# A gated mix of linear and softmax attention: where the heads' kv enters the output's weights

## The chip, the cores and the metric

The kernel runs on one core of a Trainium2 chip. The metric is the device time of one execution in microseconds (us), the median of several. The engines are TensorE (PE in the profile, with its weight loads as PEld), VectorE (DVE), ScalarE (ACT), GpSimd (POOL) and SyncE (SP), which issues every DMA of this kernel. A matmul multiplies a stationary operand, which a weight load puts into the array, with a moving operand of up to 512 columns, and writes one bank of PSUM (128 partitions by 512 numbers; there are eight).

## The reference

One input x of 2048 rows and 1024 columns goes through two attention blocks with 32 heads of 32 columns each, and a gate mixes the results:

```python
phi = lambda t: jnp.where(t > 0, t + 1, jnp.exp(t)) + 1e-6
# A: linear attention
kv = einsum("bhsd,bhse->bhde", phi(k), v)          # one 32x32 matrix for each head
z  = einsum("bhsd->bhd", phi(k))
a  = (einsum("bhqd,bhde->bhqe", phi(q), kv) / den) @ A_wo,   den = phi(q) . z + 1e-6
# B: softmax attention
b  = (softmax(q k^T * 32**-0.5) v) @ B_wo
g  = sigmoid((x * gate_w).sum(-1))
out = g * a + (1 - g) * b
```

In block A each head's kv stands between phi(q) and 32 rows of A_wo. So kv times those rows of A_wo is a matrix of weights that can be made once, and phi(q), divided by den and times g, is multiplied with it. Both the kernel before and the changed one do that. These weights are called the output's weights below: 1024 x 1024, made of 8 blocks of 128 rows (k), each holding four heads, in two halves of 512 columns (c).

## The kernel before

**Precision.** A large product is made of three: each operand is split into a high part (hi) rounded to fp32r and the rest (lo), and `three` (L145 to L150) issues hi*hi, hi*lo and lo*hi. ScalarE makes hi with a copy and VectorE or GpSimd makes lo with a subtraction. A few small products take plain fp32 instead, in one call.

**Stages.** First the value columns of B for half of the heads, then q and k of B for all heads, stored in DRAM (to L415), with the gate beside them (`gate`, L368, through the tile kvb) and x's parts spilled to DRAM. From there four streams share TensorE:

- `heads_` with `attend` (L868, L931): for each head 16 blocks of 128 keys by 4 column groups of 512 queries. A step is one product of scores (L902) and an exponential on ScalarE (L906). Groups of 5, 5 and 6 blocks are then multiplied with v (`av`, L982; L994: four matmuls for each block, whose outputs lie in four 32-partition groups of bank 4), and sums of the exponentials are kept by GpSimd (L951) and VectorE (L960).
- `maxima` (L738): the same scores in the other orientation (L752), whose row maxima VectorE takes (L757), about one head ahead.
- `linear` (L580): block A, in units of one 128-row tile with one chunk of columns: chunks v (the rest of B's values), kv (four), q (two) and o (two). A unit is 8 k-steps of three matmuls (L148 to L150). It yields to the other streams between matmuls. x's parts for a q unit or the q results (oA) for an o unit are loaded two units ahead (`load_xp`).
- `output` (L1078): block B's output product, at the end.

**Order.** The order on every engine is written out by hand: a planner in the kernel's own Python keeps a clock for each engine (`T`, with costs such as `MM` and `AV`), asks each stream when it could start, and advances the one that can start and is furthest behind. Six banks (`RING`) are handed out by `take` and `give`; VectorE work is deferred (`defer`) and filled in where the plan sees room (`fill`). `rates` (L1119 to L1125) paces `linear` against the heads' steps from the estimated cost of its chunks. SP takes the DMAs in the order of that plan and waits at each for what it depends on.

**The output's weights.** In the last unit of a chunk (tile NT-1) the weights of the next are put in place, k by k, as soon as the three matmuls on the old ones are issued: `split_w` (L444). For a q chunk they are loaded and split. For an o chunk `split_w` takes a bank, multiplies the block-diagonal 128x128 tile of four heads' kv with 128 rows of A_wo as one plain fp32 matmul (L455), copies hi from the bank (L457) and subtracts lo (L458), straight into the weights' place. That is 8 times in each of two hand-overs, from q to o and between the two o chunks. kv is summed in mid[8] during the kv chunks (`keys`, L493) and copied into the block-diagonal kvb by GpSimd after the last tile (L518), over zeros written at L635.

Of the kernel before, what the change touches and what calls it, by code (L numbers as in the profile page):

```python
# [9 lines left out]
F32 = mybir.dt.float32  # L10
# [35 lines left out]
def kernel(  # L46
# [35 lines left out]
    def f32r(ap):  # L82
# [13 lines left out]
    v_d = [dram.tile([P, NT, C], F32, name=f"v{c}") for c in range(NQC)]  # L96
    ra_d = [dram.tile([P, D], F32, name=f"ra{t}") for t in range(NT)]

    ident = sb.tile([P, P], F32, name="ident")
# [263 lines left out]

    HD = D // 2
    nc.sync.dma_start(zrep, bass.AP(tensor=gate_w.tensor, offset=gate_w.offset, ap=[[0, P], [1, D]]))
    kv_flat = kvb.rearrange("p k c -> p (k c)")

    def gate():  # L368
        for t in range(NT):
            for i in range(2):  # L370
                xn, junk = kv_flat[:, :HD], kv_flat[:, HD:]
# [51 lines left out]
    w_left = [[] for _ in range(NK)]  # L423
    xp_ready = [0.0, 0.0]
    oh, ol = f32r(mid[8]), f32r(mid[9])
    o_left = []
    k_left = []
    lin_done = [0.0]
    lin_kind = [chunks[0][0]]
# [1 line left out]
    def lin_pe(cost, *after):  # L431
        lin_done[0] += cost
        return use("pe", cost * MM, *after)

    def load_w(kind, c, k, n):
        if kind == "v":
            raw = load_cols(b_wqkv, vcols(c), k, n)
        elif kind == "kv":
            raw = load_cols(a_wqkv, [(D + c * HC, HC), (2 * D + c * HC, HC)], k, n)
        else:  # L440
            raw = load_cols(a_wqkv if kind == "q" else a_wo, [(c * C, C)], k, n)
        return raw, T["pe"] + 4.0

    def split_w(kind, c, k, raw, at, eng):  # L444

        hi, lo = wpart(k, 0), wpart(k, 1)
        w_left[k].clear()
        if kind == "o":
            yield from keys_alone(len(units))
            need(k_left)  # L450
            yield lambda: both(bank_at(), at)
            b = take()
            pb = bank[b]
            end = lin_pe(4.0, free[b])
            nc.tensor.matmul(pb, kvb[:, k, :], raw, start=True, stop=True)  # L455
            end = use("act", 0.5, end)
            nc.scalar.copy(hi, pb)  # L457
            item = defer(lambda _: nc.vector.tensor_sub(lo, pb, f32(hi)), end)  # L458
            give(b, 0.0, [item])
            w_left[k].append(item)  # L460
            return
        end = use("act", 0.52, at, T["pe"] + LATENCY["pe"])
        nc.scalar.copy(hi, raw)
        w_ready[k] = use("dve", 0.6, end) if eng is nc.vector else use("pool", 1.23, end)
        eng.tensor_sub(lo, raw, f32(hi))  # L465
# [22 lines left out]

    GC = HC // P
    kv_todo = deque()  # L490
    kv_acc = mid[8][:, :NK * DH].rearrange("p (k d) -> p k d", d=DH)

    def keys(n, c, t, pk, va, todo):  # L493

        def products(b, at):
            need(todo)
            lin_done[0] += 1.0
            end = use("pe", KV)  # L500
            pb = bank[b][:, at * GC * DH:(at + 1) * GC * DH]
            for g in range(GC):
                for r in range(4):
                    sl = slice(g * P + r * DH, g * P + (r + 1) * DH)
                    nc.tensor.matmul(pb[r * DH:(r + 1) * DH, g * DH:(g + 1) * DH], va[:, sl], pk[:, sl],  # L505
                                     start=True, stop=True)
            acc = kv_acc[:, c * GC:(c + 1) * GC, :]

            def total(_):
                part = pb.rearrange("p (k d) -> p k d", d=DH)  # L510
                if t == 0:
                    nc.vector.tensor_copy(acc, part)
                else:
                    nc.vector.tensor_add(acc, part, acc)
                if t == NT - 1:
                    for r in range(4):
                        rows = slice(r * DH, (r + 1) * DH)
                        nc.gpsimd.tensor_copy(kvb[rows, c * GC:(c + 1) * GC, rows], acc[rows])  # L518
# [16 lines left out]
    def keys_alone(n):  # L535

        while kv_todo and kv_todo[0][0] <= n:
            yield lambda: both(kv_todo[0][1](), bank_at()) if kv_todo else 0.0
            if kv_todo and kv_todo[0][0] <= n:
                use("pe", AV_SWITCH, kv_todo[0][1]())  # L540
                keys_now(T["pe"])

    z_end = [0.0, 0.0]

# [12 lines left out]
    def queries(n, c, t, pq, todo):  # L557
# [9 lines left out]
        end = use("act", 0.5, end)  # L567
        nc.scalar.copy(oh, pt)

        def low(_):  # L570
            nc.vector.tensor_sub(ol, pt, f32(oh))
            for p, src in enumerate((oh, ol)):
                nc.sync.dma_start(oA_d[p][t][:, c * TPC:(c + 1) * TPC, :],
                                  f32(src).rearrange("p (k c) -> p k c", c=P))
# [5 lines left out]
    def linear():  # L580
# [4 lines left out]
        for n, (i, t) in enumerate(units):  # L585
            kind, c = chunks[i]
            follow = chunks[i + 1] if i + 1 < len(chunks) else None
            xp = xp_t[n % 2]
            yield bank_at
# [10 lines left out]
            for k in range(NK):  # L600
# [3 lines left out]
                for m, _ in enumerate(three(ps, stat, (wpart(k, 0), wpart(k, 1)), k)):  # L604
                    lin_pe(1.0)
                    if m < 2:
                        yield always
                if k == 0 and kind == "v" and c == NQC - 1 and NT - 4 < t < NT - 1:
                    load_xp(n + 3)
                if k == 0 and n + 7 == len(units) and not o_main[0]:  # L610
# [4 lines left out]
                    split_o(1, slice(0, NK - 1))  # L615
                if k == NK - 1:
                    yield from extra
                if follow and t == NT - 2 and k < min(LEAD_W, NK):
                    coming_w.append(load_w(*follow, k, LEAD_W + 1))
                if follow and t == NT - 1:  # L620
                    yield from split_w(*follow, k, *coming_w.popleft(), nc.vector if kind == "v" else nc.gpsimd)
                    if k + LEAD_W < NK:
                        coming_w.append(load_w(*follow, k + LEAD_W, LEAD_W + 1))
            if n + 2 < len(units):
                load_xp(n + 2)
            extra = iter(())
# [4 lines left out]
            elif kind == "kv":  # L631
                va = mid[7][:, (n % 2) * HC:(n % 2 + 1) * HC]
                yield from keys_alone(n - 2)
                if c == t == 0:
                    nc.gpsimd.memset(kvb, 0.0)  # L635
# [18 lines left out]
            elif kind == "q":  # L654
# [17 lines left out]
                def divide(_, t=t, e=e, ps=ps, d=d):  # L672
# [9 lines left out]
                tasks.append((lambda todo=todo: both(ended(todo + o_left), bank_at()),  # L682
                              lambda n=n, c=c, t=t, e=e, todo=todo: queries(n, c, t, e, todo)))
            else:
                res = mid[8 + n % 2]
                give(b, use("act", 0.5, T["pe"] + LATENCY["pe"]))
                nc.scalar.copy(res, ps)
                nc.sync.dma_start(ra_d[t][:, c * C:(c + 1) * C], res)
        over["lin"] = True
        load_all()  # L690

# [176 lines left out]
    def heads_():  # L868
        pr_t.extend(big_tile(i, F32) for i in PR[:NPR])
        lacc_t.extend(big_tile(i, F32) for i in LACC)  # L870
        spare = big_tile(SPARE, F32)
        raws[2:6] = [spare[:, i * C:(i + 1) * C] for i in range(4)]
        o_ring.append(spare)
        o_ring.extend(pr_t[slot(H - 1, t)] for t in (NT - 5, NT - 3, NT - 2, NT - 1))
        tail = None
# [55 lines left out]
    def attend(h, lacc):  # L931
# [50 lines left out]
        def av(t0, t1):  # L982
# [5 lines left out]
                ends.pop()[1]()  # L988
            if bank_at() is not None and bank_at() <= T["pe"]:
                keys_now(T["pe"])  # L990
            end = use("pe", AV * len(blocks_))
            for t in blocks_:
                for j in range(NJ):
                    nc.tensor.matmul(av_b[j * DH:(j + 1) * DH, :], v[:, t, :], pr(t)[:, j * C:(j + 1) * C],  # L994
                                     start=(t == 0), stop=(t == NT - 1))
# [82 lines left out]
    def output():  # L1078
# [30 lines left out]
        for n in range(NT):  # L1109
# [124 lines left out]
```

## Time and profile before

| | us |
|---|---|
| median of 3 runs | 2902.55 (2902.52 to 2904.67) |
| the profiled execution | 2902.3 |
| its span, first to last instruction | 2900.5 |
| granted TensorE clock, mean | 0.999 |

The profile is of one execution; time outside its span is 1.8 us. The two hand-overs to o chunks lie at 2132.7 to 2154 us and 2431 to 2461 us (L455's first and last weight loads start at 2132.7 and 2460.3 us). The q chunks run from about 1720 to 2155 us, the o chunks from there to about 2720 us; after that only block B's output is left. In the profile's lines "x2" counts records of an instruction, and a plain fp32 matmul leaves two. Busy times of matmuls overlap, so costs on TensorE are read from one start to the next.

### The profile page before, as it was taken

The numbers are of one execution on the slowest core, as the hardware profiler recorded it, in microseconds if no ns is written. First come the engines' busy times: TensorE is split into PE (matmuls) and PEld (weight loads), VectorE is DVE, ScalarE is ACT, GpSimd is POOL, SyncE is SP. The second block draws the span as 40 slices with busy tenths as digits, with TensorE's granted clock in tenths as the row PEclk, the third lists the DMA queues.
The fourth block names the chain that finished last, engine by engine and source line by source line (L and its number), as shares of the span: only waits on it lengthen the run. The fifth ranks groups of instructions, "written<-read, shape, count | busy, mean of one in ns | idle before, by whom it ended". The sixth has DMA issues, their size and how long they took to land.

```text
span 2900.5 us, 43785 instructions
## 1 busy us (share of the span) xinstructions
PE 2888.7 (100%) x15840; PEld 2076.8 (72%) x15840; DVE 2057.6 (71%) x3451; ACT 1522.4 (52%) x2840; POOL 1775.7 (61%) x599
## 2 busy tenths in 40 slices
PE   9999999999999999999999999999999999999999
PEld 8888888766666666767667667676666666666787
DVE  3222114888888888888888888888887888886622
ACT  4111111466666667666766666666566666666410
POOL 0000001388898889888898896787769887786000
PEclk9999999999999999999999999999999999999999
DMA  6687333322343224222333334545443334323542
GB/s 196 211 268 236 120 124 102 115 88 89 90 125 98 90 89 119 93 88 91 117 90 95 100 117 139 157 151 160 138 151 104 105 107 130 100 88 120 197 154 78
DMA packets 273309, 364.88 MB, mean 126 GB/s; under 512 B 91146, under 2 KB 167434, under 8 KB 269962
## 3 DMA queue, kind: packets, MB, share of 16 engines
q1 hardware_dynamic: 273092, 362.07, 40.6%
q8 instruction: 125, 2.05, 0.3%
q14 instruction: 92, 0.75, 0.1%
HBM read 260.31 MB, written 100.40 MB: 124 GB/s over the span
## 4 chain that ended last, share of the span: by engine, by line
PE 97%; POOL 1%; DMA 1%; DVE 1%; issue 0%; ACT 0%; SPq 0%; POOLq 0%; ACTq 0%
PE bank L902 16%; PE bank L148 16%; PE bank L150 16%; PE bank L149 16%; PE bank L752 16%; PE bank L994 15%; PE bank L805 1%; POOL big L951 1%; PE bank L566 1%; PE bank L505 0%; DVE mx L757 0%; PE bank L455 0%; DMA mid<-in_a_wqkv 0%; POOL big L465 0%; DMA mid<-in_xT 0%
## 5 line engine op out<-in xcount | busy, mean ns | idle before, releaser
L951 POOL TENSOR_TENSOR big<-big,big 128x1536 f32<-128x1536 f32 (+1 forms) x434 | 1556.7, 3587 | 188.0 <-ACT big L906 165.5
L757 DVE TENSOR_REDUCE mx<-bank 128x1 f32<-128x512 f32 x2048 | 1312.9, 681 | 318.4 <-PE bank L752 314.5
L906 ACT ACTIVATE big<-bank 128x512 f32<-128x512 f32 x2048 | 1181.5, 601 | 525.6 <-PE bank L902 455.9
L902 PE MATMUL bank<-big,big 128*128 128x512 f32 x2048 | 811.6, 398 | 1.1 <-DMA big<-ml 0.5
L752 PE MATMUL bank<-big,big 128*128 128x512 f32 x2048 | 807.9, 395 | 3.8 <-ACT big L906 2.5
L148 PE MATMUL bank<-big,big 128*128 128x512 f32 x2048 | 801.3, 391 | 1.5 <-ACT big L254 1.4
L150 PE MATMUL bank<-big,big 128*128 128x512 f32 x2048 | 799.2, 390 | 0.0
L149 PE MATMUL bank<-big,big 128*128 128x512 f32 x2048 | 799.1, 390 | 0.0
L902 PEld LDWEIGHTS bank<-big,big 128*128 128x128 f32 x2048 | 384.0, 188 | 164.5 <-issue 67.8
L994 PE MATMUL bank<-big,mid 128*32 128x512 f32 x4096 | 458.5, 593 | 0.0
L752 PEld LDWEIGHTS bank<-big,big 128*128 128x128 f32 x2048 | 384.8, 188 | 93.4 <-ACT big L906 6.2
L148 PEld LDWEIGHTS bank<-big,big 128*128 128x128 f32 x2048 | 384.8, 188 | 87.8 <-DVE mx L757 3.0
L149 PEld LDWEIGHTS bank<-big,big 128*128 128x128 f32 x2048 | 384.8, 188 | 80.1 <-issue 0.8
L150 PEld LDWEIGHTS bank<-big,big 128*128 128x128 f32 x2048 | 384.8, 188 | 79.7 <-DVE big L255 0.6
L707 POOL MEMSET big<- 32x2048 f32 x3 | 5.4, 1808 | 530.7 <-PE bank L149 459.6
L994 PEld LDWEIGHTS bank<-big,mid 128*32 128x32 f32 x4096 | 129.0, 110 | 262.4 <-issue 262.4
L960 DVE TENSOR_TENSOR bank<-bank,big 128x512 f32<-128x512 f32 (+1 forms) x434 | 280.8, 647 | 10.0 <-ACT big L906 8.0
L255 DVE TENSOR_TENSOR mid<-bank,mid 128x512 fp32r<-128x512 f32 x64 | 44.3, 692 | 264.6 <-ACT mid L254 264.6
L947 POOL TENSOR_TENSOR big<-big,big 128x1536 f32<-128x1536 f32 (+1 forms) x31 | 111.6, 3599 | 139.8 <-ACT big L906 139.8
L254 ACT CAST mid<-bank 128x512 fp32r<-128x512 f32 x64 | 37.6, 587 | 291.6 <-PE bank L150 262.5
L812 DVE RECIPROCAL bank<-bank 128x128 f32<-128x128 f32 x128 | 123.3, 963 | 3.3 <-PE bank L805 0.3
L255 DVE TENSOR_TENSOR big<-mid,big 128x512 fp32r<-128x512 f32 x96 | 64.2, 687 | 74.7 <-ACT big L254 74.5
(76 smaller groups left out, 998.0 us busy)
## 6 DMA issues: line engine op xcount, KB each, us to landing
big<-xs SPq DMA_DIRECT2D x192, 512.0 KB, 4.1
qk<-mid SPq DMA_DIRECT2D x128, 256.0 KB, 2.8
big<-oA SPq DMA_DIRECT2D x64, 512.0 KB, 4.1
big<-qk SPq DMA_DIRECT2D x96, 256.0 KB, 4.5
big<-qk SPq DMA_DIRECT2D x384, 64.0 KB, 2.0
xs<-big SPq DMA_DIRECT2D x64, 256.0 KB, 4.2
oA<-mid SPq DMA_DIRECT2D x64, 256.0 KB, 2.8
mid<-in_b_wqkv SPq DMA_DIRECT2D x48, 256.0 KB, 3.9
```

The lines of the kernel that those rows point to most:

```text
L148: yield nc.tensor.matmul(ps, sh, mh_, start=(kt == 0), stop=False)
L149: yield nc.tensor.matmul(ps, sh, ml_, start=False, stop=False)
L150: yield nc.tensor.matmul(ps, sl, mh_, start=False, stop=(kt == NK - 1))
L752: nc.tensor.matmul(bank[b], q[:, t * P:(t + 1) * P], k[:, j * C:(j + 1) * C], start=True, stop=True)
L757: nc.vector.tensor_reduce(m[:, t, j:j + 1], bank[b], AX.X, ALU.max)
L812: nc.vector.reciprocal(pl[:, sl], pl[:, sl])
L902: nc.tensor.matmul(bank[b], k[:, t * P:(t + 1) * P], q[:, j * C:(j + 1) * C], start=True, stop=True)
L906: nc.scalar.activation(pr_t[i][:, j * C:(j + 1) * C], bank[b], AF.Exp, scale=SCALE)
L947: nc.gpsimd.tensor_add(lacc[:, :qp], pr(0)[:, :qp], pr(1)[:, :qp])
L951: nc.gpsimd.tensor_add(lacc[:, :qp], lacc[:, :qp], pr(t)[:, :qp])
L960: nc.vector.tensor_add(lacc[:, qp:] if t == NT - 1 else l_b[:, :n], l_b[:, :n], src)
L994: nc.tensor.matmul(av_b[j * DH:(j + 1) * DH, :], v[:, t, :], pr(t)[:, j * C:(j + 1) * C], start=(t == 0), stop=(t == NT - 1))
```

## The change

kv is no longer spread into block-diagonal form. kvb keeps only the 32x32 matrices (128 partitions by 8 blocks by 32 columns), and the kv sums go there directly; GpSimd's zeroing and copies are gone. The gate's scratch moves from kvb to big[20], a tile of the heads' sums that is not yet in use then.

The output's weights are made ahead of the hand-over, in four mixes, each of four blocks (half `a`) with one column half `c`. `load_mix` (called at the start of the units (q,0), (q,1) and (o,0) for tile 2 and (o,0) for tile 8) loads four 128x512 pieces of A_wo. `mix` runs between two blocks of `av`, from the group's third block on, when the plan sees the kv sums complete and four of the six banks free: 16 plain fp32 matmuls of a 32x32 kv matrix with 32 rows of A_wo, each on its own 32x32 tile of the array. Head r of each block reads partitions 32r and writes bank r; block i writes partitions 32i of it. ScalarE copies hi from each of the four banks, VectorE subtracts lo. Both parts go to DRAM in 32 stores of 32 x 512 numbers (64 KB each), two at each k-step of `linear` (`store_mix`). In the last unit ahead of an o chunk `load_wa` loads hi and lo of block k (two DMAs of 256 KB) from DRAM into the weights' place, as soon as the old weights have been used.

Beside that: weights that follow the v chunk are split two k-steps later than before (`lag`); the next q task waits until 3 us after the last low part (`o_free`); `linear` waits at a hand-over until the mix and its stores are issued; results of o units go through mid[7] and mid[10] instead of mid[8] and mid[9]; `av` counts its blocks' ends singly; and the o chunks' estimated cost loses its 4 x 8 matmuls for each half, which lowers the pace of `linear` in kv and o.

```diff
-    kvb = sb.tile([P, NK, P], F32, name="kvb")
+    kvb = sb.tile([P, NK, DH], F32, name="kvb")
...
+    def load_wa(c, k):
+        for p in range(2):
+            nc.sync.dma_start(f32(wpart(k, p)), wa_d[p][k // HK][c][k % HK])
+        w_ready[k] = T["pe"] + 5.0
...
-        if kind == "o":
-            yield from keys_alone(len(units))
-            need(k_left)
-            yield lambda: both(bank_at(), at)
-            b = take()
-            pb = bank[b]
-            end = lin_pe(4.0, free[b])
-            nc.tensor.matmul(pb, kvb[:, k, :], raw, start=True, stop=True)
-            end = use("act", 0.5, end)
-            nc.scalar.copy(hi, pb)
-            item = defer(lambda _: nc.vector.tensor_sub(lo, pb, f32(hi)), end)
...
-                if t == NT - 1:
-                    for r in range(4):
-                        rows = slice(r * DH, (r + 1) * DH)
-                        nc.gpsimd.tensor_copy(kvb[rows, c * GC:(c + 1) * GC, rows], acc[rows])
...
+    def load_mix():
+        a, c = mix_todo.popleft()
+        for i in range(HK):
+            nc.sync.dma_start(mix_hi[i], a_wo[(a * HK + i) * P:(a * HK + i + 1) * P, c * C:(c + 1) * C])
+        mix_here.append((a, c, T["pe"] + 8.0))
+    def store_mix():
+        for _ in range(min(2, len(stores))):
+            p, a, c, r, i, src = stores.popleft()
+            nc.sync.dma_start(wa_d[p][a][c][i, r * DH:(r + 1) * DH, :], f32(src[i * DH:(i + 1) * DH, :]))
+            mixed.append((a, c))
+    def mix_ready():
+        times = [ended(readers[b], free[b]) for b in RING if not held[b]]
+        return (mix_here and not kv_todo and ended(k_left, mix_here[0][2]) is not None
+                and ended(k_left, mix_here[0][2]) <= T["pe"]
+                and sum(at is not None and at <= T["pe"] for at in times) >= 4)
+    def mix():
+        a, c, _ = mix_here.pop()
+        need(k_left)
+        bs = [take() for _ in range(4)]
+        end = use("pe", AV + 0.2)
+        for r in range(4):
+            rows = slice(r * DH, (r + 1) * DH)
+            for i in range(HK):
+                nc.tensor.matmul(bank[bs[r]][i * DH:(i + 1) * DH, :], kvb[rows, a * HK + i, :], mix_hi[i][rows, :],
+                                 start=True, stop=True)
+        for r in range(4):
+            hi, lo, pb = f32r(mix_hi[r]), f32r(mix_lo[r]), bank[bs[r]]
+            at = use("act", 0.5, end)
+            nc.scalar.copy(hi, pb)
+            def low(_, r=r, hi=hi, lo=lo, pb=pb):
+                nc.vector.tensor_sub(lo, pb, f32(hi))
+                stores.extend((p, a, c, r, i, src) for p, src in enumerate((hi, lo)) for i in range(HK))
+            give(bs[r], 0.0, [defer(low, at)])
...
+            if (kind, c, t) in (("q", 0, 2), ("q", 1, 2), ("o", 0, 2), ("o", 0, 8)):
+                load_mix()
...
+                if follow and follow[0] == "o":
+                    if t == NT - 1:
+                        w_left[k].clear()
+                        yield lambda: 0.0 if mixed.count((k // HK, follow[1])) == 8 * HK else None
+                        load_wa(follow[1], k)
+                    continue
...
-            end = use("pe", AV * len(blocks_))
             for t in blocks_:
+                if mix_here:
+                    fill(T["pe"])
+                    if t - t0 > 1 and mix_ready():
+                        mix()
+                end = use("pe", AV)
...
-            "o": NQC * (NT * pace + 4 * NK)}
+            "o": NQC * NT * pace}
```

More of the change, by code (lines that the diff above doesn't have):

```diff
@@ L96 @@
     v_d = [dram.tile([P, NT, C], F32, name=f"v{c}") for c in range(NQC)]
+    wa_d = [[[dram.tile([HK, P, C], F32, name=f"wa{p}_{a}_{c}") for c in range(NQC)] for a in range(NK // HK)]
+            for p in range(2)]
     ra_d = [dram.tile([P, D], F32, name=f"ra{t}") for t in range(NT)]
@@ L365 @@
     nc.sync.dma_start(zrep, bass.AP(tensor=gate_w.tensor, offset=gate_w.offset, ap=[[0, P], [1, D]]))
-    kv_flat = kvb.rearrange("p k c -> p (k c)")
+    gate_t = f32(big[LACC[1]])
     def gate():
@@ L425 @@
     oh, ol = f32r(mid[8]), f32r(mid[9])
-    o_left = []
+    o_left, o_free = [], [0.0]
     k_left = []
@@ L440, in load_w @@
         else:
-            raw = load_cols(a_wqkv if kind == "q" else a_wo, [(c * C, C)], k, n)
+            raw = load_cols(a_wqkv, [(c * C, C)], k, n)
         return raw, T["pe"] + 4.0
@@ L490 @@
     kv_todo = deque()
-    kv_acc = mid[8][:, :NK * DH].rearrange("p (k d) -> p k d", d=DH)
     def keys(n, c, t, pk, va, todo):
@@ L506, in products @@
                                      start=True, stop=True)
-            acc = kv_acc[:, c * GC:(c + 1) * GC, :]
+            acc = kvb[:, c * GC:(c + 1) * GC, :]
             def total(_):
@@ L541, in keys_alone @@
                 keys_now(T["pe"])
+    mix_todo = deque((a, c) for c in range(NQC) for a in range(NK // HK))
+    mix_here = []
+    mixed = []
+    stores = deque()
+    mix_hi, mix_lo = [], (mid[7], mid[10], mid[0], mid[1])
+    def load_mix():
+        assert not mix_here and not stores
+        a, c = mix_todo.popleft()
[30 more added lines that the diff above has]
+            give(bs[r], 0.0, [defer(low, at)])
     z_end = [0.0, 0.0]
@@ L568, in queries, with low @@
         nc.scalar.copy(oh, pt)
-        def low(_):
+        def low(end):
+            o_free[0] = end + 3.0
             nc.vector.tensor_sub(ol, pt, f32(oh))
@@ L588, in linear, with next_w @@
             xp = xp_t[n % 2]
+            lag = 2 if kind == "v" else 0
+            def next_w(k):
+                split_w(*follow, k, *coming_w.popleft(), nc.vector if kind == "v" else nc.gpsimd)
+                if k + LEAD_W < NK:
+                    coming_w.append(load_w(*follow, k + LEAD_W, LEAD_W + 1))
             yield bank_at
@@ L607, in linear @@
                         yield always
+                store_mix()
                 if k == 0 and kind == "v" and c == NQC - 1 and NT - 4 < t < NT - 1:
@@ L617, in linear @@
                     yield from extra
+                if follow and follow[0] == "o":
[4 more added lines that the diff above has]
+                    continue
+                if follow and t == NT - 2 and k == 0:
+                    yield lambda: None if mix_here or stores else 0.0
                 if follow and t == NT - 2 and k < min(LEAD_W, NK):
                     coming_w.append(load_w(*follow, k, LEAD_W + 1))
[L620 to L623, printed above, removed]
+                if follow and t == NT - 1 and k >= lag:
+                    next_w(k - lag)
             if n + 2 < len(units):
@@ L681, in linear @@
                 give(b, 0.0, todo)
-                tasks.append((lambda todo=todo: both(ended(todo + o_left), bank_at()),
+                tasks.append((lambda todo=todo: both(ended(todo + o_left), o_free[0], bank_at()),
                               lambda n=n, c=c, t=t, e=e, todo=todo: queries(n, c, t, e, todo)))
             else:
-                res = mid[8 + n % 2]
+                res = mid[(7, 10)[n % 2]]
                 give(b, use("act", 0.5, T["pe"] + LATENCY["pe"]))
@@ L688, in linear @@
                 nc.sync.dma_start(ra_d[t][:, c * C:(c + 1) * C], res)
+            if follow and follow[0] != "o" and t == NT - 1:
+                for k in range(NK - lag, NK):
+                    next_w(k)
         over["lin"] = True
@@ L872, in heads_ @@
         raws[2:6] = [spare[:, i * C:(i + 1) * C] for i in range(4)]
+        mix_hi.extend(raws[2:6])
         o_ring.append(spare)
```

8 lines of the change are left out of this document (1 added, 7 removed).

## The prediction

> **What bounds the kernel now.** I read the page first: busy time by engine, then the chain that ended last, by engine and line.
>
> ```profile
> PE 2888.7 (100%) x15840; PEld 2076.8 (72%) x15840; DVE 2057.6 (71%) x3451; ACT 1522.4 (52%) x2840; POOL 1775.7 (61%) x599
> PE 97%; POOL 1%; DMA 1%; DVE 1%; issue 0%; ACT 0%; SPq 0%; POOLq 0%; ACTq 0%
> ```
>
> TensorE is without work for 2900.5 - 2888.7 = 11.8 us in all, and 97% of the chain is its own. So time on TensorE is the price of nearly everything, and work on the other engines is free until it makes TensorE wait. Next the groups of instructions by line, for what the change takes out, and for AV, its nearest relative:
>
> ```profile
> L994 PE MATMUL bank<-big,mid 128*32 128x512 f32 x4096 | 458.5, 593 | 0.0
> L455 PE MATMUL bank<-big,kvb 128*128 128x512 f32 x22 | 11.6, 611 | 0.4 <-DVE big L458 0.4
> L455 PE MATMUL bank<-mid,kvb 128*128 128x512 f32 x10 | 5.2, 605 | 0.0
> L458 DVE TENSOR_TENSOR big<-bank,big 128x512 fp32r<-128x512 f32 x16 | 10.8, 678 | 0.0
> L457 ACT CAST big<-bank 128x512 fp32r<-128x512 f32 x16 | 9.4, 587 | 6.0 <-PE bank L455 6.0
> L518 POOL COPY kvb<-mid 32x64 f32<-32x64 f32 x16 | 3.7, 230 | 0.5
> ```
>
> 32 records of L455 are 16 matmuls. Their records overlap others, so I take their cost from the timeline of TensorE, start to start:
>
> ```profile
> 2449.27 0.39 PE L752 MATMUL bank<-big,big 128*128 128x512 f32 x1
> 2449.50 1.02 PE L455 MATMUL bank<-big,kvb 128*128 128x512 f32 x2
> 2449.96 0.80 PE L902 MATMUL bank<-big,big 128*128 128x512 f32 x1
> 2450.60 0.40 PE L752 MATMUL bank<-big,big 128*128 128x512 f32 x1
> 2450.83 0.40 PE L902 MATMUL bank<-big,big 128*128 128x512 f32 x1
> ```
>
> An ordinary matmul starts 0.23 us after the one before it (2450.60 to 2450.83). From 2449.50 to 2450.60 there are one L455 and one L902: 1.10 - 0.23 = **0.87 us for one L455**.
>
> **The change part by part.**
>
> *Removed from TensorE:* 16 x 0.87 = **13.9 us**. All of it stood on the path.
>
> *Added to TensorE:* four mixes of sixteen 32x32 products. No row shows a product on 32 partitions of input, so I bound it. The nearest is AV, four products at a time in the four column groups, with inputs on all partitions:
>
> ```profile
> 2125.78 0.39 PE L752 MATMUL bank<-big,big 128*128 128x512 f32 x1
> 2126.09 5.36 PE L994 MATMUL bank<-big,mid 128*32 128x512 f32 x48
> 2131.38 0.50 PE L902 MATMUL bank<-big,big 128*128 128x512 f32 x1
> 2131.72 0.40 PE L148 MATMUL bank<-big,big 128*128 128x512 f32 x1
> ```
>
> 48 records are six blocks. From 2126.09 to 2131.38 is 5.29 us, 0.88 for a block of four products, each of which alone is the 0.87 of L455: four run side by side. Going in and out of this form costs 2126.09 - 2125.78 - 0.23 = 0.08 ahead and 2131.72 - 2131.38 - 0.23 = 0.11 behind, and 0.1 within the group (5.29 against 24 record times of about 0.215): some 0.3 us for a pair of changes. The lower bound for a mix is a block of AV, 0.88, if all sixteen run together. If the four row groups run one after another it is 4 x 0.88 = 3.5, and with a change of form at each 4 x 1.2 = 4.8; if nothing overlaps, 16 x 0.87 = 13.9, and the four mixes cost 55.7. I take the row nearest to it, one block of AV, with a pair of changes of form (out of AV's and back) and 0.1 for issuing twelve more products: 0.88 + 0.3 + 0.1 = **1.3 us, 5.2 for four**. My reason: sixteen products of 32 partitions read no more input rows at once than AV's four of 128.
>
> For this only the Trainium skill has a measurement: "TensorE: Matmul & The Clock Gate", section "Measured speedup vs the span model", has sixteen 32x32 tiles at N=512 finish 10.6 times as fast as one after another. As an estimate from that page the mixes would cost 55.7 / 10.6 = 5.3 us and the time would come out at 2893.7; no run here shows it yet.
>
> *Copies and subtractions:* 16 of each before (L457, L458) and 16 of each after, of the same size: nothing by themselves. But the four banks of a mix come free only after them. What covers them is that ScalarE and VectorE stand idle in an AV group, first by the last hand-over, then in the q stage:
>
> ```profile
> 2131.52 0.59 ACT L1002 COPY mid<-bank 128x512 f32<-128x512 f32 x1 [5.12 <-PE bank L994]
> 2132.85 0.69 DVE L757 TENSOR_REDUCE mx<-bank 128x1 f32<-128x512 f32 x1 [5.45 <-PE bank L752]
> 2075.45 0.59 ACT L568 CAST mid<-bank 128x512 fp32r<-128x512 f32 x1 [5.42 <-PE bank L566]
> 2071.60 3.96 DVE L812 RECIPROCAL bank<-bank 128x128 f32<-128x128 f32 x4
> ```
>
> A mix stands ahead of the third block or later, so up to three of five (2.6 us) follow it. Four copies of 0.59 and the last subtraction of 0.68 take 3.0 us, so at most half a microsecond is uncovered, with two more banks free meanwhile. Without that cover (a mix ahead of the last block, or behind L812's 3.96 us) it is 2 to 3 us. I take 0.3 for each, **1 us** in all, with 0 and 10 as ends.
>
> *The hand-overs themselves* lose the waits of L455 on its bank (0.43 us, below, and 0.4 in the group) and of copies that stand in ScalarE's queue: I credit 1 us and keep 0 to 2.5.
>
> ```profile
> 2137.56 1.12 PE L455 MATMUL bank<-big,kvb 128*128 128x512 f32 x2 [0.43 <-DVE big L458]
> ```
>
> *DMAs.* Added: 16 loads of 256 KB, 128 stores of 64 KB, and 32 loads of 256 KB in place of 16. SP issues one in about 0.43 us:
>
> ```profile
> 1917.14 0.84 SPq L573 DMA_DIRECT2D oA<-mid  x2
> SPq L723 <- PE bank L902: 232.9, 40, 14.7
> big<-in_a_wqkv SPq DMA_DIRECT2D x10, 256.0 KB, 5.5
> 1928.00:2133.00 205.00, 202.76 (x1089) 141.88 (x1082) 168.94 (x297) 125.78 (x237) 156.88 (x43) 0.99 0.52 156
> 2156.00:2431.00 275.00, 274.62 (x1499) 185.51 (x1491) 230.35 (x375) 168.10 (x295) 226.94 (x64) 1.00 0.36 107
> L148 PE MATMUL bank<-big,big 128*128 128x512 f32 x129 | 50.6, 392 | 0.0
> L148 PE MATMUL bank<-big,big 128*128 128x512 f32 x120 | 47.0, 392 | 0.0
> ```
>
> (In the window rows the last two numbers are the busy share of the DMA engines and GB/s; the two L148 rows are those of 1719 to 1928 and of 2156 to 2431.) The stores are 128 x 0.43 = 55 us of SP, two at each k-step. With 8 records of L148 in a unit, a q unit takes 209 x 8 / 129 = 13 us and an o unit 275 x 8 / 120 = 18.3, so a k-step is 1.6 or 2.3 us and holds 0.86 of stores. SP mostly waits for TensorE to release a buffer (the L723 row is one of many), so it keeps up: 0 on the path. Behind a store that waits for VectorE stand the loads of x's parts and of the heads' k; they have a unit or a head of slack. The weight loads of a hand-over are 4.2 MB in one unit. They must all be there when the next unit uses block 7, some 13 + 7/8 x 18.3 = 29 us after the first may start. Other traffic in that time is 156 GB/s x 13 + 107 x 16 = 3.7 MB; 7.9 MB in 29 us is 273 GB/s, and 156 at a share of 0.52 makes 300 possible. That fits narrowly: 0, with up to 3 us late as the other end.
>
> *The rest, at nothing.* GpSimd loses 16 copies of 0.23 us, off the path. The gate's scratch has the same instructions in another tile. `o_free` makes the q task wait 3 us after its forerunner, which is a unit of 13 us away. `lag` moves ScalarE's copies behind matmuls that are surely done; the waits it can take away are small (0.7 us for TensorE in the whole trace):
>
> ```profile
> L463 ACT CAST big<-mid 128x512 fp32r<-128x512 f32 x22 | 13.8, 627 | 2.4 <-DMA mid<-in_a_wqkv 1.4 <-PE bank L148 0.7
> ```
>
> The lower pace of `linear` (768 in place of 832 units of estimated cost) moves every later instruction against the others. With TensorE full, order alone costs nothing; but where a load comes late it does, as in the q stage now (a stall, then matmuls at 0.63 us in place of 0.39):
>
> ```profile
> 1935.78 0.50 PE L752 MATMUL bank<-big,big 128*128 128x512 f32 x1 [2.19 <-ACT big L906]
> 1937.06 0.63 PE L902 MATMUL bank<-big,big 128*128 128x512 f32 x1
> ```
>
> Such a place can come or go: -4 to +4 us, taken as 0.
>
> **The sum**, against the profiled execution (2902.3; its span is 2900.5): 2902.3 - 13.9 + 5.2 + 1 - 1 = 2893.6. The median of the runs is 0.25 above that execution, so **2893.8**. Its own range is 2888 to 2897.
>
> **The rivals.**
>
> 1. *The row groups run one after another.* Place: the mixes. Each costs 3.5 to 4.8 us, 14 to 19.4 for four, so 2902.3 to 2908. Against it: AV's rows show that column groups run together; for it: no row shows row groups doing so. It takes away the gain from 3.5 us a mix on. The Trainium skill, "TensorEngine Tiling", "Key Properties", says that a change of tiling mode drains TensorE; I price that from AV's rows above, and by it alone the gain stands.
>
> 2. *Slower: `linear` halts because no mix finds four free banks.* Place: the hand-overs, where `linear` must wait for mixed weights. While it waits the heads run alone: in 2156 to 2431 us VectorE is busy 230 us for these steps, TensorE without `linear` needs 275 - 15 units x 24 x 0.23 = 192. So TensorE would idle for 16% of a halt. A halt lasts to the next AV group, some 21 us (275 us hold 552 records, 69 blocks, 13 groups): 3.4 us; it decides once halts add up to 8.7 / 0.16 = 54 us. At 90 us it is 14 us, 2908. Against it: the two idle rows above say that banks are drained early in a group; for it: `linear` always holds one bank, a q unit's chain another, so in the q stage four of six is exactly what is left.
>
> 3. *The weight loads are late, or the banks of the mixes miss their cover:* 3 us at each hand-over, or 2 for each mix, some 4 to 6 in all: 2897 to 2900. The 273 against 300 GB/s speaks for it.
>
> 4. *Products strictly in order.* Each product is two records, 0.43 us apart, on one tile. If nothing overtook, a second record would hold up the next tile: 17 x 0.43 = 7.3 us a mix, 15 us more in all than before, 2917. AV's 48 records in 5.36 us speak against it: strictly ordered they would take over 10. The Trainium skill, "TensorE: Matmul & The Clock Gate", "The mechanism", says that matmuls start and end in strict order; by that this rival would hold, unless the two records are themselves issued in alternation, which AV's rows bear out.
>
> **How the numbers follow.** The forecast's case 0.64, rival 3 0.16, rival 1 0.10, rival 2 0.08, rival 4 0.02. Runs of this kernel can tell about 0.2%, 5.8 us: faster is below 2896.7, slower above 2908.4. Faster takes nearly all of the forecast's case and a little of rival 3: 0.65. Slower takes half of rival 2, rival 4 and a part of rival 1: 0.1. The rest is 0.25. The range 2888 to 2905 leaves out most of rivals 2 and 4, half of rival 1 and the forecast's lowest corner, about 2 in 10.
>
> **What would show it.** The mixes' 128 records in four clusters, each 1.3 us from the first start to the next matmul after it, less what AV takes there; L455 gone. If a cluster takes 3.5 us or more, rival 1; over 7, rival 4. Idle time of TensorE behind the AV group that holds a mix shows banks; idle time at L148 behind a DMA in the first unit of an o chunk shows late weights; stretches without L148 to L150 ahead of a hand-over show rival 2. I am wrong too if TensorE's idle time grows by over 5 us in places that have neither a mix nor a hand-over: then the shifted order did it.

## The result, and the profile after

The changed kernel takes **2898.28 us** (median of 22 runs, 2896.03 to 2901.41) beside 2903.26 for the kernel before: a ratio of **0.9982, interval 0.9975 to 0.9988**. That is 5.0 us less, 0.17%, where 8.7 were forecast. A second series of the same kernel gave 2896.51 beside 2902.40, a ratio of 0.9980 (0.9971 to 0.9989). The direction is clear, since both intervals lie below 1, and the time lies in the range. But the gain is hardly more than half of the forecast, and by the prediction's own bound (faster is below 2896.7) it counts as no change, to which the prediction gave 0.25; it gave 0.65 to faster.

The page after, busy times and the chain by engine:

```profile
PE 2883.5 (100%) x15936; PEld 2069.6 (71%) x15936; DVE 2052.9 (71%) x3451; ACT 1519.4 (52%) x2840; POOL 1771.7 (61%) x582
PE 97%; DVE 1%; DMA 1%; ACT 0%; SPq 0%; issue 0%; ACTq 0%; DVEq 0%
```

The bound is the same. Its span is 2896.6 us, so TensorE is without work for 13.1 us, 1.3 more than before. The mixes by the groups of instructions, and the first of them on TensorE's timeline:

```profile
L567 PE MATMUL bank<-big,kvb 32*32 32x512 f32 x128 | 6.6, 599 | 0.1
```

```profile
1826.46 2.33 PE L1055 MATMUL bank<-big,mid 128*32 128x512 f32 x20
1828.72 1.16 PE L567 MATMUL bank<-big,kvb 32*32 32x512 f32 x32
1829.81 1.92 PE L1055 MATMUL bank<-big,mid 128*32 128x512 f32 x16
```

(L1055 is AV, L994 before.) AV's 20 records begin at 1826.46 and stand for two and a half blocks at 0.86, so without the mix the next would begin near 1828.6. It begins at 1829.81: **1.2 us for sixteen products**, all side by side. No row group waits for another.

What TensorE waited for from 100 to 2880 us, the first four entries of the list before and after (us in all, times, longest):

```profile
PE bank L752 <- ACT big L906: 2.5, 2, 2.2
PE bank L752 <- ACT mid L313: 1.0, 1, 1.0
PE bank L902 <- DMA big<-ml: 0.5, 1, 0.5
PE bank L455 <- DVE big L458: 0.4, 1, 0.4
```

```profile
PE bank L151 <- ACT big L257: 2.1, 1, 2.1
PE bank L808 <- DMA big<-qk: 2.0, 1, 2.0
PE bank L959 <- ACT mid L740: 1.2, 1, 1.2
PE bank L808 <- ACT mid L740: 0.6, 1, 0.6
```

The waits of before are gone or short, and four new ones have come. They are where the missing gain is looked for below. (Lines after: L151 to L153 are the three-part products, L808 and L959 the scores, L740 the copy of an o unit's result, L257 and L258 the splits, L605 the copy of a q result's hi, L550 the stores of the mixed weights, L611 those of the q results.)

The first stage, in which nothing but scratch was changed, took 1.5 us longer in the profile after (the v chunk begins at 443.3 us, before at 441.8). I therefore also compare the *middle* of each trace, from the 1921st start of a three-part product (where the v chunk begins) to the 5377th (the first product of the output). Before it is 2280.5 us, after 2274.4, and 2273.7 in the second series: 6.1 to 6.8 us less. The middle does not hold everything either: from its end to the end of the span it is 178.2 us before, and 178.9 and 180.0 us in the two profiles of the changed kernel. So 0.7 to 1.8 us of that gain are lost again behind the wait at L151. And the middle of one execution can hold a stretch of slower clock or not (last section), which moves it by 1.7 us.

### The profile page after: what moved, and what is told of

The parts are those of the page before. It is cut to its first block, busy times and chain, and to the rows that moved or that the text cites. A ratio compares the mean times of both kernels' runs of the same rounds, so it can differ in the third digit from the quotient of the medians.

```text
span 2896.6 us, 44105 instructions
## 1 busy us (share of the span) xinstructions
PE 2883.5 (100%) x15936; PEld 2069.6 (71%) x15936; DVE 2052.9 (71%) x3451; ACT 1519.4 (52%) x2840; POOL 1771.7 (61%) x582
## 4 chain that ended last, share of the span: by engine, by line
PE 97%; DVE 1%; DMA 1%; ACT 0%; SPq 0%; issue 0%; ACTq 0%; DVEq 0%
PE bank L959 16%; PE bank L808 16%; PE bank L151 16%; PE bank L153 16%; PE bank L152 16%; PE bank L1055 15%; PE bank L861 1%; PE bank L603 1%; PE bank L498 0%; DVE big L1021 0%; DMA big<-in_a_wo 0%; ACT big L963 0%; DMA ra<-mid 0%; PE bank L567 0%; ACT big L257 0%; SPq L550 0%
## 5 line engine op out<-in xcount | busy, mean ns | idle before, releaser
L959 PE MATMUL bank<-big,big 128*128 128x512 f32 x2048 | 809.6, 397 | 1.2 <-ACT mid L740 1.2
L808 PE MATMUL bank<-big,big 128*128 128x512 f32 x2048 | 802.8, 392 | 3.3 <-DMA big<-qk 2.0
L151 PE MATMUL bank<-big,big 128*128 128x512 f32 x2048 | 802.1, 392 | 3.3 <-ACT big L257 3.2
L153 PE MATMUL bank<-big,big 128*128 128x512 f32 x2048 | 799.9, 391 | 0.4 <-DVE big L258 0.4
L959 PEld LDWEIGHTS bank<-big,big 128*128 128x128 f32 x2048 | 383.8, 188 | 159.6 <-issue 61.2
L1055 PE MATMUL bank<-big,mid 128*32 128x512 f32 x4096 | 460.8, 595 | 0.0
L151 PEld LDWEIGHTS bank<-big,big 128*128 128x128 f32 x2048 | 385.1, 188 | 92.3 <-ACT big L963 4.3
L808 PEld LDWEIGHTS bank<-big,big 128*128 128x128 f32 x2048 | 384.6, 188 | 88.8 <-ACT big L963 6.4
L153 PEld LDWEIGHTS bank<-big,big 128*128 128x128 f32 x2048 | 384.9, 188 | 82.0 <-DVE big L258 1.1
L1055 PEld LDWEIGHTS bank<-big,mid 128*32 128x32 f32 x4096 | 127.7, 110 | 265.1 <-issue 265.1
L258 DVE TENSOR_TENSOR mid<-bank,mid 128x512 fp32r<-128x512 f32 x64 | 44.3, 691 | 263.1 <-ACT mid L257 263.1
L257 ACT CAST mid<-bank 128x512 fp32r<-128x512 f32 x64 | 37.6, 587 | 291.6 <-PE bank L153 277.0
L258 DVE TENSOR_TENSOR big<-mid,big 128x512 fp32r<-128x512 f32 x96 | 64.0, 687 | 77.9 <-ACT big L257 77.6
```

Of the source, the lines that this page charges most:

```text
L151: yield nc.tensor.matmul(ps, sh, mh_, start=(kt == 0), stop=False)
L153: yield nc.tensor.matmul(ps, sl, mh_, start=False, stop=(kt == NK - 1))
L808: nc.tensor.matmul(bank[b], q[:, t * P:(t + 1) * P], k[:, j * C:(j + 1) * C], start=True, stop=True)
L959: nc.tensor.matmul(bank[b], k[:, t * P:(t + 1) * P], q[:, j * C:(j + 1) * C], start=True, stop=True)
```

## The experiments

Theory 1: the products cost what was forecast, and the rest of the gain went into a few new waits on buffers and late DMAs. Theory 2: the new pace and order of the plan lost it, and single waits are taken up elsewhere. Except where the pace is changed, the variants keep the order of the products on TensorE (the last one only renames some buffers), so that they differ in one wait each. The medians are of 11 runs for c_after, e2, e3 and e4, and of 5 for the other variants.

| run | median, us | ratio to before (interval) | middle, us |
|---|---|---|---|
| changed kernel | 2898.28 | 0.9982 (0.9975 to 0.9988) | 2274.4 |
| c_after, the same again | 2896.51 | 0.9980 (0.9971 to 0.9989) | 2273.7 |
| e1_lo_buffers | 2894.47 | 0.9966 (0.9954 to 0.9979) | 2270.7 |
| e5_early_load | 2893.59 | 0.9963 (0.9950 to 0.9975) | 2269.9 |
| e2_mix_twice | 2898.92 | 0.9982 (0.9973 to 0.9991) | 2275.1 |
| e6_no_products | 2889.46 | 0.9952 (0.9938 to 0.9965) | 2267.1 |
| e8_no_stores | 2890.00 | 0.9960 (0.9947 to 0.9972) | 2266.4 |
| e9_single_stores | 2889.17 | 0.9955 (0.9941 to 0.9969) | 2265.1 |
| e10_all | 2886.79 | 0.9943 (0.9930 to 0.9956) | 2263.1 |
| e3_old_pace | 2899.38 | 0.9992 (0.9983 to 1.0000) | see there |
| e4_before_new_pace | 2901.30 | 1.0002 (0.9993 to 1.0011) | 2278.5 |

**The control.**

> The changed kernel once more, as a control beside the others. All theories: 2898.3, within 1.5 us.

It was 2896.51, 1.8 us lower and outside the 1.5 expected, with the kernel before 0.9 us lower as well. Medians of different series differ that much, so I read ratios and traces.

**Other buffers for the low parts.**

```diff
-            hi, lo, pb = f32r(mix_hi[r]), f32r(mix_lo[r]), bank[bs[r]]
+            hi, lo, pb = f32r(mix_hi[r]), f32r((mix_lo if c == 0 else (mid[3], mid[4], mid[0], mid[1]))[r]), bank[bs[r]]
```

> The changed kernel with the two late mixes' low parts in mid[3] and mid[4] in place of mid[7] and mid[10]; the order of every engine stays as it is. Theory 1 (the results' buffers): in the changed kernel ScalarE's copy of an o unit's result waited 1.55 and 0.85 us for stores of low parts out of the same buffers, and TensorE 1.15 and 0.6 us behind it (with the refill some 2 us). Those waits go and the time falls by 1.5 to 2 us, to about 2896.5. Theory 2 (order): such waits are taken up elsewhere, what was lost against the forecast is lost by the new order of the plan; the time stays within 0.5 us of 2898.3.

The ground for it were these rows of the changed kernel's ScalarE and TensorE, 13 us after the start of the third mix:

```profile
2228.51 0.58 ACT L740 COPY mid<-bank 128x512 f32<-128x512 f32 x1 [1.55 <-DMA wa<-mid]
```

```profile
2229.15 0.50 PE L959 MATMUL bank<-big,big 128*128 128x512 f32 x1 [1.15 <-ACT mid L740]
```

The change keeps two of the mix's four low parts in mid[7] and mid[10], whose stores are among the 32 that go out over two units, and puts the o units' results into the same two. So ScalarE stands at the copy of a result until a store of low parts has left its buffer, exponentials queue behind it, and TensorE runs out of free banks. With other buffers both waits are gone from the list, the middle is 3.0 to 3.7 us shorter and the ratio falls from 0.9982 to 0.9966 (the intervals overlap a little). This is more than the 1.5 to 2 expected: theory 1, with the price too low. The two waits are 1.8 us of TensorE in this profile and 2.4 in that of the control; the rest of the difference I cannot place.

**A_wo's pieces for the fourth mix one unit earlier.**

```diff
+            if (kind, c, t) == ('o', 0, 7): [nc.sync.dma_start(mix_hi[i], a_wo[(HK + i) * P:(HK + i + 1) * P, C:]) for i in range(HK)]
...
-        for i in range(HK):
+        for i in range(HK if (a, c) != (1, 1) else 0):
```

> As the run with the other low buffers, and the loads of A_wo for the fourth mix are issued one unit earlier; the order of TensorE, VectorE, ScalarE and GpSimd stays as it is. Theory 1: the fourth mix's 1.5 us of waiting for these loads goes as well: another 1.5 us less than with the buffers alone, about 2895, and the four mixes all cost 1.2 to 1.5 us. Theory 2: at most 0.5 us.

In the changed kernel the fourth mix takes 2.8 us from its first record to the next AV, beside 1.1 for the first mix. Its rows by SP, TensorE and the weight loads:

```profile
2319.24 3.48 SPq L544 DMA_DIRECT2D big<-in_a_wo  x4
```

```profile
2326.40 2.89 PE L567 MATMUL bank<-big,kvb 32*32 32x512 f32 x32
...
2329.23 1.92 PE L1055 MATMUL bank<-big,mid 128*32 128x512 f32 x16
```

```profile
2328.16 0.23 PEld L567 LDWEIGHTS bank<-big,kvb 32*32 32x32 f32 x26 [0.97 <-DMA big<-in_a_wo]
```

SP issued the four loads from 2319.2 to 2322.7. The plan counts 8 us for them from where it has TensorE at the call; the mix began at 2326.40, and the last load landed at about 2328.1, 1.7 us later. With the early load all four mixes take 1.2 us in the trace. The middle fell by 0.8 us and the ratio by 0.0003, less than the 1.5 expected, and less than the medians' differences can show; only the trace shows this wait gone.

**The products twice, and not at all.**

```diff
-        for r in range(4):
+        for r in [0, 1, 2, 3] * 2:
```

> The changed kernel with the sixteen products of each mix issued twice, in the same place and order, with no second change of form. Side by side (what the first profile shows): 0.86 us more for each mix, 3.4 us in all, about 2901.7. Row groups one after another: 4 x 3.4 = 14 us more, 2912. Strictly in order, 29 us more.

> The changed kernel without the 64 products of the mixes: the copies, subtractions, stores and loads stay, and so does the order; the output's weights are then made of what lay in the banks, so block A's result is wrong. Theory 1: the mixes' products cost 4 x 1.2 plus 1.5 to 1.8 us of waiting for loads, 6.5 us: about 2891.8. If the products were the whole of what is missing from the forecast, 9 us less: 2889. If they overlapped with AV and cost nearly nothing, 2897.

Sixteen more products on the same tiles cost 1.2 us, not 0.86: from 1826.72 to the next AV at 1829.00 are 2.28 us, beside 1.09 in the single mix.

```profile
1826.72 2.35 PE L567 MATMUL bank<-big,kvb 32*32 32x512 f32 x64
1829.00 1.92 PE L1055 MATMUL bank<-big,mid 128*32 128x512 f32 x16
```

That is 4.8 us on TensorE's timeline, but the middle grew by only 0.7 to 1.4 and the ratio not at all, for two reasons. The wait on L740 fell from 1.8 us in all to 0.4 when the o chunk's mixes moved against the results. And the middle of this execution has no stretch of slower clock, where both profiles of the changed kernel have one, of 1.7 us. Row groups in turn (14 us) and strict order (29 us) are both excluded. Without the products (and with whatever lay in the banks as weights) the middle is 6.6 to 7.3 us shorter. Theory 1 expected 6.5, and the rows of the four mixes, late loads included, add up to 6.7 (1.09, 1.09, 1.36 and 2.82 us to the next AV, and 0.09 ahead of each). By the medians it is 8.8, which is nearer to the 9 of the second expectation; medians of different series do not separate the two.

**Old pace, new pace.**

```diff
-            "o": NQC * NT * pace}
+            "o": NQC * (NT * pace + 4 * NK)}
```

> The changed kernel with the old estimate of the o chunks' cost, so with the old pace of the linear stream in kv and o. Theory 1 (the missing gain lies in two waits on buffers and loads): the pace is worth little, 2898 with 2 us either way. Theory 2 (the new order lost what is missing): with the old pace the order is nearer to the kernel before, and the time falls by 2 to 4 us, to 2895.

> The kernel before with the new, lower estimate of the o chunks' cost and nothing else. Theory 1: 2903 with 2 us either way. Theory 2: the new pace alone makes the kernel before slower by 2 to 4 us, 2906.

Theory 2 falls as far as the pace goes. With the old pace the changed kernel gets slower, 2.9 us by the medians beside the control of the same series (ratio 0.9992; the intervals overlap a little): the linear stream is through before the heads are, and TensorE is left with scores that ScalarE's exponentials hold up:

```profile
2704.49 2.71 PE L959 MATMUL bank<-big,big 128*128 128x512 f32 x7
2707.70 1.97 PE L959 MATMUL bank<-big,big 128*128 128x512 f32 x4 [0.50 <-ACT big L963]
```

The new pace belongs to the change, then. The kernel before does not care about it (1.0002). In that run the first q result takes mid[8] ahead of the last addition of kv, which stands there too, so block A's result is wrong and only the time is read; in the changed kernel the sums have a place of their own.

**No stores; then one store at each k-step.** After the two buffers one wait in the q stage was left, named "DMA big<-qk" in the list. The kernel with the early load, SP and ScalarE around it:

```profile
2017.76 1.84 SPq L550 DMA_DIRECT2D wa<-big  x4
2019.64 2.04 SPq L550 DMA_DIRECT2D wa<-mid  x4
2021.79 0.97 SPq L473 DMA_DIRECT2D big<-xs  x2
2022.82 0.90 SPq L611 DMA_DIRECT2D oA<-mid  x2
```

```profile
2028.44 0.58 ACT L605 CAST mid<-bank 128x512 fp32r<-128x512 f32 x1 [3.41 <-DMA oA<-mid]
...
2029.13 1.08 ACT L963 ACTIVATE big<-bank 128x512 f32<-128x512 f32 x2
```

```profile
2029.78 0.50 PE L808 MATMUL bank<-big,big 128*128 128x512 f32 x1 [1.92 <-DMA big<-qk]
```

The q result's low part was ready at 2020.57 (L609 began at 2019.89 and took 0.68), but SP had eight stores of mixed weights to issue first, back to back to 2021.7, and two loads of x's parts behind them. The result's stores went out from 2022.82; the next q task's copy into the same buffer stood 3.4 us; the exponential that frees TensorE's bank ended at 2029.72; TensorE starts at 2029.78. So the releaser is ScalarE, and the name in the list is not the cause.

> The kernel with the other low buffers and the early load, without the 128 stores of the mixed weights; the weights of the o chunks are loaded from another stored tile of the same shape, so block A's result is wrong. The order of the computing engines stays. Theory 1: the stores are hidden behind SP's waits and cost 0 to 0.5 us: 2893.5. A rival, that SP or the DMA engines are crowded by them: 2 us or more less, 2891.

```diff
-        for _ in range(min(2, len(stores))):
+        for _ in range(min(1, len(stores))):
```

> The kernel with the other low buffers and the early load, with one store of the mixed weights at each k-step in place of two; the order of the computing engines stays. Theory 1a (SP is crowded in the q stage by two stores at each k-step, so that the q results' store goes out 2 us late and the next q task's copy waits for its buffer): TensorE's wait of 2 us behind that copy, near 2025 us, goes, with the slower clock after it: 2 to 3.5 us less than with two stores, about 2890.5. A rival, that it is the DMA engines' load and not SP's turn: the same bytes go out in the same stage, so the wait stays and the time is within 1 us of 2893.6.

Without stores the wait is gone and the middle is 3.5 us shorter (by the ratio 0.0003, not to be told apart): the rival in that expectation is right and my 0 to 0.5 us wrong. With all of the stores, but one at a time, the wait is gone as well and the middle 4.8 us shorter, the ratio 0.9955, its interval overlapping that of two at a time. Of both differences 1.7 us are the slower clock, which follows the wait in e5. So it was SP's turn, not the bytes. The landing says the same: from the first of the result's two stores to the next copy into its buffer it is 5.6 us with the wait, and 5.5 both without stores and with single ones. SP in this run, with the q results' store (L611) at 2017.45 between the others:

```profile
2013.77 1.83 SPq L550 DMA_DIRECT2D wa<-mid  x4
2015.64 0.42 SPq L550 DMA_DIRECT2D wa<-big  x1
2016.58 0.81 SPq L473 DMA_DIRECT2D big<-xs  x2
2017.45 0.90 SPq L611 DMA_DIRECT2D oA<-mid  x2
2018.39 3.08 SPq L550 DMA_DIRECT2D wa<-big  x3
```

**B_wo's last pieces earlier, with everything else.**

```diff
-    wo_raws = [mid[i] for i in (0, 1, 3, 4, 5, 6)]
+    wo_raws = [mid[i] for i in (0, 1, 3, 4, 5, 6, 8, 9)]
...
                 if last and t >= WO_SLOT:
-                    wo_load()
+                    [wo_load() for _ in range(3 if t == NT - 1 else 1)]
```

> As the run with single stores, and the last two pieces of B_wo are loaded with the last head's last block, through two more raw buffers (mid[8], mid[9]). Theory: the changed kernel and all its variants lose 2 to 3 us at the end of the linear stream, near 2710 us, because ScalarE's splits of these pieces stand waiting ahead of the split that the first output product needs; that wait goes: 2 to 3 us less again, about 2888. If the wait only moves to the next link (the sums of the last head on VectorE), within 1 us of the run with single stores.

The longest wait of the changed kernel, at the end of the linear stream:

```profile
2715.66 1.14 ACT L257 CAST big<-mid 128x512 fp32r<-128x512 f32 x2 [6.92 <-DMA mid<-in_b_wo]
2716.71 1.78 ACT L257 CAST big<-big 128x896 fp32r<-128x896 f32 x2
```

```profile
2717.69 0.50 PE L151 MATMUL bank<-big,big 128*128 128x512 f32 x1 [2.09 <-ACT big L257]
```

The output's first product needs the second of these splits, which stands on ScalarE behind two whose data were issued late. With these loads issued earlier the wait is gone. This is all that TensorE still waited for in this run by the list, from 100 to 2880 us:

```profile
PE bank L808 <- ACT big L963: 0.3, 1, 0.3
```

The median is 2886.79 beside 2902.16 for the kernel before, 0.9943 (0.9930 to 0.9956): 2.4 us less than with single stores, as expected, and the fastest of all.

## Why the prediction was right or wrong

- **What was removed and added on TensorE: right.** L455 is gone, sixteen products cost 1.2 us where 1.3 was forecast, and four undisturbed mixes (e5) take 4.8 us where 5.2 was. The clusters and their length were the sign named ahead. Rivals 1 and 4 are excluded: sixteen first records start within 0.12 us and only then, 0.45 us behind the first, the second ones. Taken product by product, the strict order that the Trainium skill states in "TensorE: Matmul & The Clock Gate", "The mechanism", does not hold here. Whether the records were already issued in this alternation, as the prediction allowed, no run shows.
- **The banks of a mix: right, and cheaper.** Apart from the loads TensorE never waited behind an AV group with a mix; of the 1 us put there nothing was needed. Rival 2 did not occur either: the second mix began at 1996.45 us, more than 160 us ahead of the first load of mixed weights, and `linear` never stood for one.
- **The hand-overs' weight loads: right.** Nobody waits for them. The sum asked for 273 GB/s over 29 us; in the 29 us from 2159 on it is 276, and in the 18 us from 2160 on 322 with the DMA engines 0.97 busy. So it fits narrowly, as said, with the limit above the 300 of the estimate:

```profile
2160.00:2178.00 18.00, 18.00 (x102) 11.89 (x101) 13.48 (x25) 10.18 (x20) 12.98 (x5) 1.00 0.97 322
```

- **The step that failed is "SP mostly waits for TensorE to release a buffer (the L723 row is one of many), so it keeps up: 0 on the path", with "Behind a store that waits for VectorE stand the loads of x's parts and of the heads' k; they have a unit or a head of slack".** I asked what loads are late behind the new stores and left out the stores: the q results' own store stands there as well, its buffer is single, and the next q task comes within a unit. SP keeps up over a unit and not over 10 us. Price: the 2 us wait and, in some executions, 1.7 us of slower clock after it; 3.5 to 4.8 us by the middles. The buffer is a weak place without the new stores too: in the kernel before with the new pace (e4) the same copy waits 2.02 us near 1939 us, and TensorE 1.33 behind it.
- **A part that was not costed at all:** the results' move to mid[7] and mid[10] stands in the description of the change and in no term of the sum. Price: 1.8 to 2.4 us of TensorE's waiting, 3.0 to 3.7 us by the middles, shown by e1.
- **The late loads of A_wo:** 8 us were taken for enough; the fourth mix waited 1.5 us or more. Shown by e5's trace, not by its time.
- **"Such a place can come or go: -4 to +4 us, taken as 0":** both happened. The stall of 2.19 us at 1935.78 does not appear after; with the old pace (e3) the changed kernel has it again, 2.15 us at 1935.21, and not the one near 2029 us. And a stall of 2.1 us at the end of the linear stream is there after, up to e10. It is neither in e3 nor in e4, so it takes the change and the new pace together; what in the order puts it there is not shown, and e10 shows only that earlier loads remove it. The sign named for this, idle time grown by over 5 us, did not show: it grew by 1.3, because old waits went as new ones of 5.9 us came.

With the late load and the shared buffers gone (e5) the ratio is 0.9963, 10.7 us below before, and with the stores' crowding gone too 13; forecast were 8.7. So the sum was also too high in its other terms, and that the time came out within the range is in part luck: new waits, put at nothing, met waits of before that went, credited with 1 us. The traces place most of it. TensorE's idle time in the middle is 5.5 us before, 6.6 after and 0.3 in e10. From before to after 13.9 removed, less 6.7 for the mixes with their late loads and 1.1 of idle time, is 6.1, which is what the middles differ by. In e10 the mixes take 5.0, and 5.2 us of idle time and the 1.7 us of slower clock behind the old stall are gone: 15.8 of 17.4 us. No run places the other 1.6.

## What to carry to other kernels

When work is taken off the bound engine and turned into DMAs, list for each new DMA the buffer that it holds and who writes that buffer next, and for the queue that issues it what else must go out in the same 10 us, stores included: one copy that waits for its buffer on an in-order engine holds up everything behind it. A small gain that is missing is found by reading the bound engine's list of waits against that of before and removing one wait at a time without touching the order. And the name in that list is the last semaphore, not always the cause: look at what ended just ahead of the start.

## What the runs showed of the hardware

A wait of TensorE of about two us can be followed by some us of slower clock, and need not be. In the run with the early load the granted clock in the 6 us after the wait is 0.72, which costs about 1.7 us (6 x 0.28). In the control, with 2.16 us of the same wait up to 2027.69, it is 1.00; in the run with single stores, without the wait, it is 1.00 as well:

```profile
2029.00:2035.00 6.00, 5.22 (x28) 1.81 (x32) 3.13 (x6) 1.81 (x5) 4.00 (x1) 0.72 0.87 245
```

```profile
2027.00:2033.00 6.00, 5.31 (x44) 2.00 (x48) 3.12 (x6) 1.72 (x4) 4.02 (x1) 1.00 0.85 244
```

```profile
2029.00:2035.00 6.00, 6.00 (x40) 3.71 (x32) 2.58 (x4) 3.69 (x7) 0.53 (x1) 1.00 1.10 196
```

The Trainium skill, "TensorE: Matmul & The Clock Gate", section "HAM oscillation — how this bites in real kernels", gives about 3.4 us of idling as the limit; here a wait of 1.92 us was enough. Of the 19 waits of 1.5 to 2.3 us behind the first stage in the twelve traces, 11 were followed by such a stretch; what decides it no run here shows. Where it came, removing the wait brought 1.7 us more than its length. The middles of before, after, c_after, e1, e5 and e6 hold one stretch each, those of e2, e4, e8, e9 and e10 none.

The first stage differs in length from one execution to the next, whatever the kernel (441.5 to 443.5 us in the twelve traces): in its second 6 us TensorE has 24 matmuls in the profile of before and 18 in that of after, and the rest of the stage keeps a distance of 1.5 us. In the profile of after the three-part products start 0.43 us apart up to 10.0 us, in that of before 0.23 us apart from 7.2 us on. What decides it stays open.

```profile
6.00:12.00 6.00, 5.84 (x24) 4.53 (x25) 4.56 (x7) 4.35 (x8) 0.00 (x0) 1.00 0.84 281
```

```profile
6.00:12.00 6.00, 6.00 (x18) 4.73 (x19) 4.64 (x8) 4.34 (x7) 0.00 (x0) 1.00 0.82 257
```
